# Block-sparse attention with a feed-forward layer on one core: the first eight steps in a new order, weights converted four pieces a step, and the score transposes on TensorE for eight steps and not fourteen

## The chip, the cores and the metric

The kernel runs on one core of one Trainium2 chip. The metric is the device time of one execution in microseconds (us); a kernel's time is the median of its runs. PE is TensorE, DVE is VectorE, ACT is ScalarE, POOL is GpSimd and SP is SyncE, as in the profile.

## The reference

Attention over 4 batches, 8 heads, 768 positions and head size 64, with a mask in blocks of 32, and behind it a layer norm and a two-layer feed-forward with a residual:

```python
scores = (q @ k.T) / sqrt(64)                      # per batch and head, 768 x 768
mask   = |block_i - block_j| <= 1, or block 0 or 23 on either side,
         or one of three sampled blocks of row block i
attn   = softmax(where(mask, scores, -1e9))
x      = (attn @ v), heads side by side            # 4 x 768 x 512, float32
xn     = (x - mean) / sqrt(var + 1e-6) * g_ln
out    = x + relu(xn @ w_ch1) @ w_ch2              # 512 -> 2048 -> 512, weights arrive as float64
```

## The kernel before, in words

**Precision.** Matrix products are made of 16-bit pairs: each operand is split into a rounded high part and the rest as a low part (high by ACT, low by DVE), and three products stand for one: high by high, low by high, high by low.

**Steps.** The attention is cut into 64 steps, 16 for each batch. A sparse step takes one tile of 128 query rows and four heads: scores against 8 key blocks for each row block (`scores`, L324, 96 matmuls). A dense step (16 of the 64) does the row blocks 0 and 23, which see all keys (`dense_scores`, L355, 16 matmuls). Step i then runs: row maximum on DVE (`softmax_max`, L368), exponentials on ACT (`softmax_exp`, L377), a transpose of the 128 x 1024 probabilities, their split in high (ACT, L387) and low (DVE, L394), and the product with V (`attn_v` L431 or `dense_v` L458, called P by V here, 96 or 72 matmuls), whose result DVE divides by the row sums (`finish`, L415 to L418). Steps below `NPE` are early: they are transposed by eight (dense: six) matmuls on PE (`turn`, L382) inside the PSUM tile `ps` that held the scores. Later steps round first (L389, L396) and are transposed by two DMAs on SP's queue (L398), and their P by V is issued `LAG` = 2 steps later. `ps` has two buffers.

**Units.** Twelve units of two query tiles go through `ffn`: 192 matmuls up (L523, 24 for one pair of hidden tiles in PSUM tile `pu`), relu and rounding of a pair on ACT (L531, `hh`) and the rest on DVE (L532, `hl`), then 96 matmuls down (L541, `pd`). `ffn` is a generator: `run(n)` issues its next n pieces, so its matmuls are strewn between the steps' own. Unit 0 holds steps 0 to 3, unit 1 steps 4 to 7, unit 2 steps 8 to 15. A unit is queued behind the one before it.

**Weights.** Both weight matrices come once, in 32 pieces of 512 KB of float64 bits (16 of w1, 16 of w2). `convert_w` makes a piece float32 with three integer operations on DVE (L173, L175, L177, tile `wf`), then rounds it on ACT (`high()`, L187) and forms the low part on DVE (`low()`, L182). Raw pieces wait in three buffers of the pool `raw` or, by the table `HOME`, in eight places inside the final tiles `w2h` and `w2l`, which are filled last. `WPOS` says at which place of which step a piece is converted. `ffn` of unit 0 goes on only with pieces that were written before the step began (`wready`).

**Order.** Nothing is scheduled by a tool: each engine does its instructions in the order in which the code issues them, and an instruction that waits holds all behind it on that engine. The loop at the end writes the order by hand. `hook(i, p)` does what was registered for place p of step i (conversions, gathers) and then lets SP load what is due within ten places. `gather_v` loads the rows of V of a step by DMAs of SP (L290, L294) and up to four indirect ones of POOL (L298); it waits until the buffer `vg` of three steps before has been read by P by V. `gather_k` copies sampled key blocks on ACT (L281). The keys and values of the next batch are converted in steps 7 to 13 (L227, L228, L241, L242).

In an early step the order before is: exponentials of step i, scores of step i+1, feed-forward pieces, `finish` of step i-1, transposes of step i, maximum of step i+1, high and low of step i, P by V of step i. Each early step converts two pieces, or three from step 8 on.

Of the kernel before, what the change touches and what calls it, by code (L numbers as in the profile page):

```python
# [26 lines left out]
def sparse_attention_moe(  # L27
# [28 lines left out]

    ORDER = ((1, 2), (3, 4), (0, 5))
    LAG, FFLAG = 2, 2
    NPE, XPE = 14, 2
    FFU = 192 + 2 * 16 * 6  # L60

    const = ctx.enter_context(tc.tile_pool(name="const", bufs=1))
# [94 lines left out]
    def load_w(i):  # L157
        wraw[i] = stage(i)
        nc.sync.dma_start(wraw[i], weight(i)[0].bitcast(I32))
# [348 lines left out]


    def ffn(u):  # L510
        xT = u.xT
        hh = hp.tile([P, FT, 2 * P], F16, tag="hh", name=f"hh{u.i}")
        hl = hp.tile([P, FT, 2 * P], F16, tag="hl", name=f"hl{u.i}")
        for f in range(0, FT, 2):
            ph = ps_f.tile([P, 512], F32, tag="pf", name=f"pu{u.i}_{f}")
            for j in range(2):
                fs = slice((f + j) * P, (f + j + 1) * P)
                n = 0
                for c in range(CT):
                    for w, k in ((w1h, 0), (w1l, 0), (w1h, 1)):  # L520
                        while u.i == 0 and f // 4 * CT + c not in wready:
                            yield True
                        nc.tensor.matmul(ph[:, j * 2 * P : (j + 1) * 2 * P], w[:, c, fs],  # L523
                                         xT[:, c, k, :], start=n == 0 and j == 0,
                                         stop=n == 3 * CT - 1, skip_group_check=True)
                        n += 1
                        if n < 3 * CT or j == 0:
                            yield
            dh = hh[:, f : f + 2, :].rearrange("p f n -> p (f n)")
            dl = hl[:, f : f + 2, :].rearrange("p f n -> p (f n)")  # L530
            nc.scalar.activation(dh, ph, AF.Relu)  # L531
            nc.vector.scalar_tensor_tensor(out=dl, in0=ph, scalar=0.0, in1=dh,  # L532
                                           op0=ALU.max, op1=ALU.subtract)
            yield

        def down(po, k, f):
            while u.i == 0 and NW1 + f not in wready:
                yield True
            cols = slice(k * P, (k + 1) * P)
            for n, (x, w) in enumerate(((hh, w2h), (hh, w2l), (hl, w2h))):  # L540
                nc.tensor.matmul(po, x[:, f, cols], w[:, f, :], start=f == 0 and n == 0,  # L541
                                 stop=f == FT - 1 and n == 2)

        def store(po, k):
            t = u.ts[k]
            ot = wfp.tile([P, DM], F32, tag="wf", name=f"ot{u.i}_{k}")
            nc.vector.scalar_tensor_tensor(out=ot, in0=po, scalar=1.0 / (SW1 * SW2),
                                           in1=xs[u.b, t], op0=ALU.mult, op1=ALU.add)
            nc.sync.dma_start(out[u.b, t * P : (t + 1) * P, :], ot)

        po = [ps_f.tile([P, DM], F32, tag="pf", name=f"pd{u.i}_{k}") for k in range(2)] if u.i == 0 else []
        if u.i == 0:
            for f in range(FT):
                for k in range(2):
                    yield from down(po[k], k, f)
                    for _ in range(6):
                        yield
            for k in range(2):
                store(po[k], k)
        else:  # L560
            for k in range(2):
                p = ps_f.tile([P, DM], F32, tag="pf", name=f"pd{u.i}_{k}")
                for f in range(FT):
                    yield from down(p, k, f)
                    if f < FT - 1:
                        for _ in range(6):
# [29 lines left out]

    POS = ("pre", "a", "b", "c", "d", "e", "f")
    LEAD = 10

    def place(n):  # L600
        return n + (1 if n < NPE else LAG)

    def matmul_scores(s):
        (dense_scores if s.dense else scores)(s)
# [80 lines left out]
    gather_k(steps[0])  # L685
    for kt in range(3, NT):
        convert_v(0, kt)
    at(0, "a", lambda: convert_k(0, 1, 0))
    at(0, "b", lambda: convert_k(0, 1, 1))
    at(0, "b", lambda: convert_q(0, first[1]))  # L690

    WPOS = [(0, "f")] + [(i, p) for i in range(1, 8) for p in "ab"]
    for i in range(8, 16):
        WPOS += [(i, p) for p in "abf"]
    WPOS = WPOS[:NW]
    assert len(WPOS) == NW
    for i, (n, p) in enumerate(WPOS):
        if i < 3:
            def first_w(i=i):
                convert_w(i)  # L700
                busy["raw"] -= 1
            at(n, p, first_w)
        else:
            item(n, p, HOME.get(i, "raw"), lambda i=i: load_w(i), lambda i=i: convert_w(i))
    for b in range(1, B):
        f = next(s.i for s in steps if s.b == b)
        for kt in range(NT):
# [40 lines left out]
    avail = {}  # L748
    for u in units:
        last = max(s.i for s in steps if s.u is u)  # L750
        avail[u.i] = last + 2 if last < NPE else last + LAG + FFLAG
    need = 0
    i = 0
    tail = None
    while i < NS + LAG + FFLAG + 1 or ffq:
        s = steps[i] if i < NS else None
        for u in units:
# [8 lines left out]
        if i < NPE:  # L766
            if i == 0:
                matmul_scores(s)
                softmax_max(s)
            softmax_exp(s)  # L770
            ahead = 0 < i < NPE - 1
            if ahead:
                matmul_scores(steps[i + 1])
            need -= run(part[0] + part[1])
            hook(i, "a")
            lns = []
            if tail:
                tail()
                lns = norms(steps[i - 1])
            for x in lns:  # L780
                next(x)
            high()
            turn(s)
            if i == 0:
                hook(i, "b")
                keys(1)
            keys(i + 2)
            need -= run(part[2])
            if ahead:
                softmax_max(steps[i + 1])  # L790
            for x in lns:
                next(x)
            hook(i, "b")
            need -= run(part[3])
            split_high(s)
            low()
            for x in lns:
                next(x, 0)
            hook(i, "c")
            split_low(s)  # L800
            high()
            hook(i, "d")
            need -= run(part[4] + part[5])
            tail = matmul_values(s)
            if i == 0:
                matmul_scores(steps[i + 1])
                softmax_max(steps[i + 1])
            hook(i, "e")
            need -= run(part[6])
            low()  # L810
            hook(i, "f")
            high()
            need -= run(part[7])
        else:
            if s:
                matmul_scores(s)
            need -= run(part[0])
            lns = []
            if tail:
                tail()  # L820
                lns = norms(steps[i - 1])
                tail = None
            if s:
                softmax_max(s)
            low()
            hook(i, "a")
            need -= run(part[1])
            if s:
                softmax_exp(s)
            high()  # L830
            need -= run(part[2])
            low()
            hook(i, "b")
            if s:
# [24 lines left out]
            high()  # L859
            need -= run(part[7])  # L860
            low()
# [67 lines left out]
```

## Time and profile before

| | |
|---|---|
| runs | 916.3, 919.24 and 1111.67 us, median 919.24 us |
| profiled execution | 922.66 us, span of its instructions 920.9 us |
| PE busy | 744.5 us (81% of the span) |
| DVE busy | 497.7 us (54%) |
| ACT busy | 468.8 us (51%) |
| DMA moved | 134.08 MB |

The busy shares are means over stages with different limits. The page's second part has the span in 40 slices of 23 us: PE nearly fills its slices from about 253 us on, and does not before. A step is read off the trace by the start of its row maximum (L368 on DVE), the one instruction that each step has once; these starts are the bounds of the windows that the prediction uses.

### The profile page before, as it was taken

What the parts mean: (1) busy time and instruction counts of PE and PEld (TensorE: products, weight loads), DVE (VectorE), ACT (ScalarE), POOL (GpSimd) and SP (SyncE); (2) the same over time, 40 slices, a digit from 0 to 9 for tenths busy, and PEclk for the clock granted to TensorE, in tenths of its full rate; (3) what the DMA queues carried; (4) which work ended last, traced back from release to release, by engine and by line L of the source; (5) the groups of instructions that cost most, each with busy time, mean ns of one, the idle gap of its engine ahead of it and who ended that gap; (6) DMA issues with size and microseconds to landing.
All of it is one profiled execution on the core that took longest, in us unless ns stands there. A gap on an engine that the chain in (4) does not pass through costs nothing.

```text
span 920.9 us, 31832 instructions
## 1 busy us (share of the span) xinstructions
PE 744.5 (81%) x13816; PEld 499.1 (54%) x13816; DVE 497.7 (54%) x900; ACT 468.8 (51%) x1201; POOL 171.8 (19%) x187
## 2 busy tenths in 40 slices
PE   1255584566598899999797899998787999999898
PEld 0133463443366485766554666756544847577483
DVE  4366556889735554554655454546654456435420
ACT  5545434445446565453776565536764664435120
POOL 0522301102001322120222331112122320201000
PEclk9997587787689999999988999999977999999999
DMA  8746632546535887777757887877487785656300
GB/s 286 197 139 186 169 119 90 149 147 206 154 92 106 160 155 168 135 181 176 201 109 163 155 149 174 169 181 195 101 168 165 146 149 138 118 112 123 70 1 23
DMA packets 185419, 134.08 MB, mean 146 GB/s; under 512 B 128960, under 2 KB 164288, under 8 KB 185280
## 3 DMA queue, kind: packets, MB, share of 16 engines
q1 hardware_dynamic: 175872, 108.07, 50.8%
q0 software_dynamic: 8448, 23.44, 10.3%
q8 instruction: 108, 1.77, 0.8%
q10 hardware_dynamic: 960, 0.54, 0.2%
q14 instruction: 31, 0.25, 0.1%
HBM read 89.18 MB, written 12.95 MB: 111 GB/s over the span
## 4 chain that ended last, share of the span: by engine, by line
PE 59%; DVE 13%; issue 8%; ACT 5%; DMA 2%; ACTq 0%; SPq 0%; DVEq 0%
PE pd L541 26%; PE pu L523 21%; PE ps L324 6%; PE pa L431 4%; DVE st L368 2%; DVE hl L532 2%; ACT kg L281 2%; DVE kx L228 1%; DVE wf L175 1%; ACT ps L377 1%; PE pd L458 1%; DVE wf L177 1%; PE ps L355 1%; DVE w2l L182 1%; DMA w2l<-w 1%
## 5 line engine op out<-in xcount | busy, mean ns | idle before, releaser
L298 POOL DMA_INDIRECT vg<-vdr,vidx x176 | 171.2, 973 | 664.7 <-PE pa L431 443.1
L523 PE MATMUL pu<-xT,w1h 128*128 128x256 f16 x1536 | 272.7, 279 | 4.5 <-DVE hl L532 1.8
L523 PE MATMUL pu<-xT,w1l 128*128 128x256 f16 x768 | 214.6, 279 | 0.0
L523 PEld LDWEIGHTS <-w1h 128*128 128x128 f16 x1536 | 153.8, 100 | 30.7 <-issue 4.1
L541 PE MATMUL pd<-w2h,hh 128*128 128x512 f16 x384 | 152.6, 397 | 0.0
L541 PE MATMUL pd<-w2l,hh 128*128 128x512 f16 x384 | 151.5, 394 | 0.0
L541 PE MATMUL pd<-w2h,hl 128*128 128x512 f16 x384 | 150.8, 393 | 0.0
L377 ACT ACTIVATE ps<-ps,st 128x256 f32<-128x256 f32 (+1 forms) x164 | 78.6, 479 | 136.4 <-DVE st L369 132.3
L532 DVE SCALAR_TENSOR_TENSOR hl<-pu,hh 128x512 f16<-128x512 f32 x96 | 65.3, 688 | 111.0 <-ACT hh L531 92.1
L541 PEld LDWEIGHTS <-hh 128*128 128x128 f16 x768 | 73.1, 101 | 88.4 <-issue 13.6
L531 ACT ACTIVATE hh<-pu 128x512 f16<-128x512 f32 x96 | 55.8, 592 | 126.9 <-PE pu L523 107.3
L281 ACT COPY kg<-kx 128x128 f16 x576 | 119.2, 294 | 1.9 <-issue 0.8
L396 DVE TENSOR_TENSOR pw<-ps,pw 128x1024 f16<-128x1024 f32 (+1 forms) x50 | 58.0, 1161 | 106.9 <-ACT pw L389 99.7
L368 DVE TENSOR_REDUCE st<-ps 128x4 f32<-128x1024 f32 (+1 forms) x64 | 73.7, 1151 | 62.9 <-PE ps L324 62.7
L431 PE MATMUL pa<-vg,pt 128*32 128x65 f16 (+1 forms) x4224 | 54.4, 204 | 52.2 <-DVE pt L394 26.4
L431 PEld LDWEIGHTS <-pt 128*32 128x32 f16 x4224 | 45.4, 101 | 71.5 <-DVE pt L394 27.7
L523 PEld LDWEIGHTS <-w1l 128*128 128x128 f16 x768 | 76.9, 100 | 11.7 <-issue 2.0
L324 PEld LDWEIGHTS <-ql 64*32 64x32 f16 x2304 | 34.3, 97 | 71.5 <-issue 47.7
L324 PE MATMUL ps<-kx,ql 64*32 64x96 f16 (+1 forms) x1536 | 44.1, 211 | 35.1 <-DVE ql L265 18.1
L541 PEld LDWEIGHTS <-hl 128*128 128x128 f16 x384 | 38.9, 101 | 49.5 <-issue 7.5
L324 PE MATMUL ps<-kx,qx 128*32 128x96 f16 (+1 forms) x1536 | 45.1, 219 | 10.6 <-issue 10.4
L324 PE MATMUL ps<-kg,ql 64*32 64x96 f16 x768 | 41.4, 216 | 14.5 <-issue 11.3
(80 smaller groups left out, 737.9 us busy)
## 6 DMA issues: line engine op xcount, KB each, us to landing
vg<-vdr SPq DMA_DIRECT2D x32, 390.0 KB
w2l<-w SPq DMA_DIRECT2D x13, 512.0 KB
va<-vdr SPq DMA_DIRECT2D x8, 780.0 KB
w2h<-w SPq DMA_DIRECT2D x12, 512.0 KB
out<-ot SPq DMA_DIRECT2D x24, 256.0 KB
qr<-qs SPq DMA_DIRECT2D x22, 256.0 KB
vdr<-vs SPq DMA_DIRECT2D x36, 130.0 KB
vg<-vdr SPq DMA_DIRECT2D x16, 292.5 KB
```

The lines of the kernel that those rows point to most:

```text
L175: nc.vector.scalar_tensor_tensor(out=wf, in0=raw[:, :, 1], scalar=-0x40000000, in1=wf, op0=ALU.bitwise_and, op1=ALU.bitwise_or)
L281: nc.scalar.copy(kg[:, n], kxs[b, hg][:, :, bass.ds(val, 1)].rearrange("p j o q k -> p j (o q) k"))
L298: nc.gpsimd.indirect_dma_start(vg[:, qb - 4 * s.t, 1, :], None, src[:, :], bass.IndirectOffsetOnAxis(ap=vidx[:, qb : qb + 1], axis=0))
L324: nc.tensor.matmul(dst[:, at : at + n], stat, src[rows], start=first, stop=last, skip_group_check=True)
L368: nc.vector.tensor_reduce(out=s.st[:, 0 : s.m], in_=s.parts, axis=AX.X, op=ALU.max)
L377: nc.scalar.activation(to[:, k], s.parts[:, k], AF.Exp, bias=s.st[:, k : k + 1], scale=0.125)
L396: nc.vector.tensor_sub(s.pw[:, 1, 0 : s.n], s.whole, s.pw[:, 0, 0 : s.n])
L431: nc.tensor.matmul(pa[gr * BLK : (gr + 1) * BLK, hl * 66 : hl * 66 + n], s.pt[:, ch + c, half, gr * BLK : (gr + 1) * BLK], s.vg[:, gr, c, ...
L523: nc.tensor.matmul(ph[:, j * 2 * P : (j + 1) * 2 * P], w[:, c, fs], xT[:, c, k, :], start=n == 0 and j == 0, stop=n == 3 * CT - 1, skip_gr ...
L531: nc.scalar.activation(dh, ph, AF.Relu)
L532: nc.vector.scalar_tensor_tensor(out=dl, in0=ph, scalar=0.0, in1=dh, op0=ALU.max, op1=ALU.subtract)
L541: nc.tensor.matmul(po, x[:, f, cols], w[:, f, :], start=f == 0 and n == 0, stop=f == FT - 1 and n == 2)
```

## The change

`NPE` falls from 14 to 8, so that steps 8 to 13 are transposed by DMA and their P by V comes two steps later. In steps 0 to 7 the order is written anew: P by V of step i-1 stands in step i, behind the transposes of step i, and the scores of step i+1 stand behind that. Pieces 0 to 2 are converted inside step 0, and from step 1 on four pieces a step (places a to d), so that piece 31, the last, stands in step 8 and not in step 13. The feed-forward of unit 0 is queued at step 4, and not 5. In `ffn`, relu and low part of a pair of hidden tiles (`hidden`) are issued when the matmuls of the next pair have been.

```diff
-    NPE, XPE = 14, 2
+    NPE, XPE = 8, 2
...
-            dh = hh[:, f : f + 2, :].rearrange("p f n -> p (f n)")
-            dl = hl[:, f : f + 2, :].rearrange("p f n -> p (f n)")
-            nc.scalar.activation(dh, ph, AF.Relu)
-            nc.vector.scalar_tensor_tensor(out=dl, in0=ph, scalar=0.0, in1=dh,
-                                           op0=ALU.max, op1=ALU.subtract)
+            if late:
+                late.pop()()
+
+            def hidden(f=f, ph=ph):
+                dh = hh[:, f : f + 2, :].rearrange("p f n -> p (f n)")
+                dl = hl[:, f : f + 2, :].rearrange("p f n -> p (f n)")
+                nc.scalar.activation(dh, ph, AF.Relu)
+                nc.vector.scalar_tensor_tensor(out=dl, in0=ph, scalar=0.0, in1=dh,
+                                               op0=ALU.max, op1=ALU.subtract)
+
+            late.append(hidden)
             yield
+        late.pop()()
...
-    WPOS = [(0, "f")] + [(i, p) for i in range(1, 8) for p in "ab"]
-    for i in range(8, 16):
-        WPOS += [(i, p) for p in "abf"]
+    WPOS = [None] * 3 + [(i, p) for i in range(1, 9) for p in PAT.get(i, "abcd")]
...
-        avail[u.i] = last + 2 if last < NPE else last + LAG + FFLAG
+        avail[u.i] = last + 2 - 100 * (u.i == 0) if last < NPE else last + LAG + FFLAG
...
             softmax_exp(s)
-            ahead = 0 < i < NPE - 1
-            if ahead:
-                matmul_scores(steps[i + 1])
-            need -= run(part[0] + part[1])
-            hook(i, "a")
-            lns = []
-            if tail:
+            turn(s)
+            if i == 0:
+                convert_w(0)
+                convert_k(0, 1, 0)
+                split_high(s)
...
+            else:
+                hook(i, "a")
+                high()
+                tail = matmul_values(steps[i - 1])
+                need -= run(part[0] + part[1])
+                hook(i, "b")
+                low()
+                split_high(s)
+                high()
+                split_low(s)
+                if i < NPE - 1:
+                    matmul_scores(steps[i + 1])
                 tail()
                 lns = norms(steps[i - 1])
-            for x in lns:
-                next(x)
-            high()
-            turn(s)
...
+                for x in lns:
+                    next(x)
+                keys(i + 2)
+                need -= run(part[2] + part[3])
+                hook(i, "c")
+                low()
+                high()
+                for x in lns:
+                    next(x)
+                if i < NPE - 1:
+                    softmax_max(steps[i + 1])
+                need -= run(part[4] + part[5])
+                hook(i, "d")
+                low()
...
+                if i == 4:
+                    ffq.append(ffn(units[0]))
+                    need += FFU
+                    need -= run(24)
+                need -= run(part[6] + part[7])
```

Three places show what this does to the order of an engine. First DVE around the low part of step 3 (`pt` is the transposed probability tile, `wf` a weight piece on its way, `w1l` its low part, `st` and `ps` the maximum and scores of a step). Before:

```order
L368 TENSOR_REDUCE st_1365<-ps_1237 128x4
L369 TENSOR_SCALAR st_1365<-st_1365 128x4
L173 TENSOR_SCALAR wf_1368<-w2l 128x512
L175 SCALAR_TENSOR_TENSOR wf_1368<-w2l,wf_1368 128x512
L177 SCALAR_TENSOR_TENSOR wf_1368<-w2l,wf_1368 128x512
L182 SCALAR_TENSOR_TENSOR w1l<-wf_1334,gs,w1h 128x512
L394 TENSOR_TENSOR pt_1372<-ps_935,pt_1372 128x8x128
L182 SCALAR_TENSOR_TENSOR w1l<-wf_1368,gs,w1h 128x512
```

Now:

```order
L173 TENSOR_SCALAR wf_1191<-w2h 128x512
L175 SCALAR_TENSOR_TENSOR wf_1191<-w2h,wf_1191 128x512
L177 SCALAR_TENSOR_TENSOR wf_1191<-w2h,wf_1191 128x512
L173 TENSOR_SCALAR wf_1295<-w2l 128x512
L175 SCALAR_TENSOR_TENSOR wf_1295<-w2l,wf_1295 128x512
L177 SCALAR_TENSOR_TENSOR wf_1295<-w2l,wf_1295 128x512
L182 SCALAR_TENSOR_TENSOR w1l<-wf_1159,gs,w1h 128x512
L182 SCALAR_TENSOR_TENSOR w1l<-wf_1191,gs,w1h 128x512
L394 TENSOR_TENSOR pt_1301<-ps_997,pt_1301 128x8x128
L415 TENSOR_SCALAR rc_2_0_0_1402<-pa_1198 128x4
L416 RECIPROCAL rc_2_0_0_1402<-rc_2_0_0_1402 128x4
L418 TENSOR_TENSOR x_2_1403<-pa_1198,rc_2_0_0_1402 128x256
```

The maximum of step 4 (`st_1365` before) stands ahead of the low part of step 3 (`pt_1372` before, `pt_1301` now) before, and behind these rows now; two pieces' conversions stand directly ahead of the low part.

Second PE where the transposes of step 3 end and P by V begins (`pa` is its result). Before:

```order
L324 LDWEIGHTS qx_3_1036
L324 MATMUL ps_1237<-kg_3_0_1089,qx_3_1036 32x96
L382 MATMUL ps_935<-ident,pw_1232 128x128 x8
L431 LDWEIGHTS pt_1372
L431 MATMUL pa_1384<-vg_823,pt_1372 32x65
```

Now:

```order
L324 MATMUL ps_997<-kg_2_1_825,qx_2_437 32x96
L494 MATMUL px_1_1151<-ident,xn_1_1149 128x128 x4
L382 MATMUL ps_997<-ident,pw_1178 128x128 x8
L431 LDWEIGHTS pt_993
L431 MATMUL pa_1198<-vg_280,pt_993 32x65
```

Before, P by V reads `pt_1372`, the tile that is made from the transposes just ahead of it; now it reads `pt_993`, the tile of step 2. The scores ahead are those of step 4 before, of step 3 itself now.

Third SP from the last gather of an early step on (`va` and `vr` are values, `vdr` their place in memory, `w2l`, `w2h` and `wr` weight pieces on arrival). Before:

```order
L290 DMA vg_1988<-vdr_1_125 96x4x520
L294 DMA vg_1988<-vdr_1_125 32x4x520
L159 DMA w2l<-w 128x1024 x2
L235 DMA vr_0_2317<-v 128x512
L304 DMA va_0_2321<-vdr_0_124 128x6x520
L159 DMA w2l<-w 128x1024
L159 DMA w2h<-w 128x1024 x2
L235 DMA vr_1_2522<-v 128x512
```

Now:

```order
L290 DMA vg_2115<-vdr_1_125 96x4x520
L294 DMA vg_2115<-vdr_1_125 32x4x520
L159 DMA wr_2149<-w 128x1024
L159 DMA w2h<-w 128x1024
L159 DMA wr_2185<-w 128x1024
L159 DMA wr_2187<-w 128x1024
L159 DMA w2l<-w 128x1024
L159 DMA w2h<-w 128x1024
L304 DMA va_0_2504<-vdr_0_124 128x6x520
L235 DMA vr_0_2664<-v 128x512
L159 DMA wr_2693<-w 128x1024
```

From this place on seven weight pieces are still to come now, all shown; before, 19 were, of which five are shown. Each of them waits on SP for the place it is loaded into, and the gathers and value loads stand behind it.

More of the change, by code (lines that the diff above doesn't have):

```diff
@@ L510, in ffn @@
     def ffn(u):
-        xT = u.xT
+        xT, late = u.xT, []
         hh = hp.tile([P, FT, 2 * P], F16, tag="hh", name=f"hh{u.i}")
@@ L598, in sparse_attention_moe @@
     LEAD = 10
+    PAT = {}
     def place(n):
@@ L687, in sparse_attention_moe @@
         convert_v(0, kt)
-    at(0, "a", lambda: convert_k(0, 1, 0))
-    at(0, "b", lambda: convert_k(0, 1, 1))
-    at(0, "b", lambda: convert_q(0, first[1]))
-    WPOS = [(0, "f")] + [(i, p) for i in range(1, 8) for p in "ab"]
-    for i in range(8, 16):
-        WPOS += [(i, p) for p in "abf"]
+    WPOS = [None] * 3 + [(i, p) for i in range(1, 9) for p in PAT.get(i, "abcd")]
     WPOS = WPOS[:NW]
     assert len(WPOS) == NW
[L697 to L704, printed above, removed]
+    for i, at_w in enumerate(WPOS):
+        if at_w:
+            item(*at_w, HOME.get(i, "raw"), lambda i=i: load_w(i), lambda i=i: convert_w(i))
     for b in range(1, B):
@@ L750, in sparse_attention_moe @@
         last = max(s.i for s in steps if s.u is u)
-        avail[u.i] = last + 2 if last < NPE else last + LAG + FFLAG
+        avail[u.i] = last + 2 - 100 * (u.i == 0) if last < NPE else last + LAG + FFLAG
     need = 0
     i = 0
-    tail = None
     while i < NS + LAG + FFLAG + 1 or ffq:
@@ L770, in sparse_attention_moe @@
             softmax_exp(s)
-            ahead = 0 < i < NPE - 1
-            if ahead:
-                matmul_scores(steps[i + 1])
-            need -= run(part[0] + part[1])
-            hook(i, "a")
-            lns = []
-            if tail:
+            turn(s)
[5 more added lines that the diff above has]
+                split_low(s)
+                convert_k(0, 1, 1)
+                keys(1)
+                convert_w(1)
+                convert_q(0, first[1])
+                low()
+                matmul_scores(steps[1])
+                high()
+                convert_w(2)
+                keys(2)
+                softmax_max(steps[1])
+                low()
+                busy["raw"] = 0
+            else:
[6 more added lines that the diff above has]
+                split_high(s)
+                high()
+                split_low(s)
+                if i < NPE - 1:
+                    matmul_scores(steps[i + 1])
@@ L778, in sparse_attention_moe @@
                 tail()
                 lns = norms(steps[i - 1])
-            for x in lns:
-                next(x)
-            high()
-            turn(s)
[L784 to L813, printed above, removed]
+                for x in lns:
+                    next(x)
@@ new lines, in sparse_attention_moe @@
+                keys(i + 2)
+                need -= run(part[2] + part[3])
+                hook(i, "c")
+                low()
+                high()
+                for x in lns:
[4 more added lines that the diff above has]
+                hook(i, "d")
+                low()
+                for x in lns:
+                    next(x, 0)
+                if i == 4:
+                    ffq.append(ffn(units[0]))
+                    need += FFU
+                    need -= run(24)
@@ L814, in sparse_attention_moe @@
+                need -= run(part[6] + part[7])
+                hook(i, "e")
+                hook(i, "f")
         else:
@@ L818, in sparse_attention_moe @@
             lns = []
-            if tail:
-                tail()
+            if i == NPE:
+                matmul_values(steps[i - 1])()
                 lns = norms(steps[i - 1])
-                tail = None
             if s:
```

## The prediction

> **What bounds the kernel now.** I read the page's slices first, then windows cut at the starts of the row maxima, then who waited for whom, then the chain. Columns of a slice row are tenths of 23 us:
>
> ```profile
> PE   1255584566598899999797899998787999999898
> DVE  4366556889735554554655454546654456435420
> PEclk9997587787689999999988999999977999999999
> ```
>
> Two stages are to be seen. From slice 12 (253 us) on PE is at 8 to 9 tenths nearly throughout and DVE at half: there the matmuls set the pace. In the eleven before, PE stands at 1 to 6 tenths but for one 8, its clock from slice 4 on below full, and DVE climbs to 8 and 9 in slices 8 to 10. The early steps and the weights lie in this part, and everything that the change reorders by hand lies ahead of step 19. The issue order behind step 19 is the same in both programs but for the roundings, so the question is when step 19 starts. The markers of steps 2, 9 and 19:
>
> ```profile
> 59.71 1.21 DVE L368 TENSOR_REDUCE st<-ps 128x4 f32<-128x1024 f32 x1
> ...
> 170.83 0.93 DVE L368 TENSOR_REDUCE st<-ps 128x1 f32<-128x768 f32 x1
> ...
> 321.33 1.23 DVE L368 TENSOR_REDUCE st<-ps 128x4 f32<-128x1024 f32 x1 [2.01 <-PE ps L324]
> ```
>
> The windows between markers (columns: bounds, length, busy time of PE, PEld, DVE, ACT, POOL with counts, clock, DMA share, GB/s) are those of steps 3, 5, 10, 11, 12, 13 and 18:
>
> ```profile
> 73.80:88.30 14.50, 8.06 (x205) 5.87 (x206) 9.01 (x17) 7.72 (x25) 3.78 (x4) 0.69 0.54 161
> ...
> 101.70:124.80 23.10, 17.33 (x266) 13.30 (x267) 9.58 (x17) 5.95 (x14) 3.78 (x4) 0.59 0.48 153
> ...
> 186.90:199.10 12.20, 7.21 (x189) 5.49 (x189) 11.78 (x25) 4.65 (x10) 0.00 (x0) 0.86 0.28 70
> 199.10:211.20 12.10, 8.30 (x116) 3.91 (x115) 11.65 (x23) 4.83 (x10) 3.26 (x3) 0.86 0.60 172
> 211.20:224.50 13.30, 8.36 (x112) 4.10 (x111) 11.51 (x23) 4.94 (x12) 2.84 (x3) 0.74 0.73 257
> 224.50:257.70 33.20, 16.74 (x275) 10.08 (x273) 23.47 (x37) 15.64 (x36) 3.98 (x4) 0.68 0.48 145
> ...
> 308.50:321.30 12.80, 11.60 (x235) 6.07 (x234) 3.96 (x7) 7.70 (x21) 3.78 (x4) 1.00 0.86 163
> ```
>
> Step 3 uses neither engine fully: 14.5 us for 9.0 of DVE and 8.1 of PE. Steps 10 to 12, with three pieces a step, are DVE's: 34.9 us busy of 37.6, or 0.93. The waits say why step 3 is loose (first two rows PE's from 0 to 321 us, the others DVE's from 24.3 to 321):
>
> ```profile
> PE pa L431 <- DVE pt L394: 26.4, 9, 4.9
> PE pd L458 <- DVE pt L394: 11.9, 4, 5.0
> ...
> DVE st L368 <- PE ps L324: 32.4, 8, 13.8
> DVE hl L532 <- ACT hh L531: 25.5, 9, 6.0
> DVE hl L532 <- issue: 13.3, 1, 13.3
> ```
>
> P by V waits for the low part of its own step (38 us), the next scores stand behind it on PE, and the maximum on DVE waits for those (32 us): one ring through both engines. The last row is one stall of 13.3 us in step 5, where ACT and DVE stood at a rounding of the feed-forward while PE still ran its pair at half clock.
>
> **The change part by part.** *P by V one step behind.* PE then has the low part ready long before it is asked for, so the two waits of 38 us go. What is late next is DVE, since four pieces a step now stand in its queue. Its prices, from the groups of the first 276 us (after the bar: busy us, mean ns):
>
> ```profile
> L368 DVE TENSOR_REDUCE st<-ps 128x4 f32<-128x1024 f32 (+1 forms) x16 | 18.4, 1149 | 29.5 <-PE ps L324 29.4
> L382 PE MATMUL ps<-ident,pw 128*128 128x128 f32 x104 | 19.0, 341 | 7.7 <-ACT pw L377 7.5
> L394 DVE TENSOR_TENSOR pt<-ps,pt 128x1024 f16<-128x1024 f32 (+1 forms) x14 | 15.9, 1139 | 5.6 <-ACT kg L281 5.6
> L182 DVE SCALAR_TENSOR_TENSOR w1l<-wf,gs,w1h 128x512 f16<-128x512 f32 x16 | 11.8, 743 | 0.0
> L177 DVE SCALAR_TENSOR_TENSOR wf<-w2h,wf 128x512 int32<-128x512 int32 x12 | 8.4, 697 | 0.4
> L532 DVE SCALAR_TENSOR_TENSOR hl<-pu,hh 128x512 f16<-128x512 f32 x10 | 6.9, 688 | 34.2 <-ACT hh L531 20.9 <-issue 13.3
> L173 DVE TENSOR_SCALAR wf<-w2l 128x512 int32<-128x512 int32 x13 | 5.4, 419 | 0.0
> L418 DVE TENSOR_TENSOR x<-pa,rc 128x256 f32<-128x256 f32 (+2 forms) x12 | 5.1, 423 | 0.4
> ```
>
> A piece costs DVE 0.42 + 2 x 0.70 + 0.74 = 2.56 us. *From the maximum of step 2 to that of step 9* the new order has on DVE: 26 triples of integer operations (1.82 each) 47.3 us, 27 low parts 20.1, seven maxima of 1.15 and as many low parts of P of 1.14 16.0, eight `hl` 5.5, and some 54 shorter ones (query parts, `finish`, norms, scalings) at the 0.42 of the last row, 22.7; together about 111 us. At the 0.93 of steps 10 to 12 that is 120 us. Before, the same stretch takes 111 (59.7 to 170.8), with 14 triples in it and not 26: so it becomes longer, not shorter.
>
> *PE in the same stretch.* All of unit 0 moves into it. Prices are read from the chain (start, us, count), at full clock:
>
> ```profile
> 282.61 4.80 PE pu L523 x43
> ...
> 290.86 2.59 PE pd L541 x12
> ```
>
> that is 0.112 us a matmul up and 0.216 down. Between the maxima of steps 6 and 8 the new order has 146 up and 51 down, 27.4 us, and twice a step's own 8.1 us (step 3's row, without feed-forward), 43.6 in all; DVE has 40.5 there, 43.6 at 0.93. The two are even, and two queues that wait for each other now and then lose a little: I add 3 us. The bounds are 0 and, with the clock at half all through, another 27.4.
>
> *Steps 0 and 1.* The scores of step 1 no longer stand behind P by V of step 0, but those of step 2 still stand behind it and the gathers. I leave the maximum of step 2 at 59.7, 8 us either way. The maximum of step 9 then stands at 59.7 + 120 + 3 = 183, against 170.8 before: 12 us are lost here.
>
> *Steps 9 to 18* have no weights any more, and unit 1 alone spread over ten steps: 192 up and 108 down, 45 us, where before units 0 and 1 are crowded into steps 14 to 18. They hold a change of batch, and the profile has two later ones with the same work by the same late code. Steps 28 to 33, then 60 and 61, which carry little feed-forward:
>
> ```profile
> 435.70:449.00 13.30, 11.29 (x237) 8.97 (x236) 9.40 (x18) 8.89 (x21) 4.67 (x5) 1.00 0.83 222
> 449.00:461.40 12.40, 7.82 (x202) 6.31 (x200) 8.56 (x17) 8.37 (x20) 1.64 (x2) 0.88 0.67 170
> 461.40:470.00 8.60, 8.60 (x207) 5.87 (x206) 3.81 (x7) 6.95 (x21) 0.48 (x1) 0.98 0.34 63
> 470.00:477.50 7.50, 5.58 (x108) 3.00 (x107) 5.34 (x13) 6.79 (x20) 3.30 (x4) 0.86 0.50 115
> 477.50:488.60 11.10, 8.35 (x192) 4.37 (x191) 4.80 (x11) 7.59 (x21) 3.78 (x4) 0.94 0.95 191
> 488.60:501.30 12.70, 10.44 (x193) 5.22 (x192) 9.24 (x19) 7.32 (x23) 3.90 (x4) 0.79 0.75 158
> ...
> 823.60:832.40 8.80, 8.80 (x155) 6.84 (x155) 4.81 (x12) 5.14 (x16) 2.84 (x3) 1.00 0.90 192
> 832.40:841.00 8.60, 7.33 (x213) 6.22 (x213) 4.64 (x12) 5.03 (x16) 2.83 (x3) 1.00 0.74 169
> ```
>
> Steps 12 to 17 by the first six: 65.6 us; steps 9, 10, 11 and 18 at 8.7: 34.8; together 100, against 150.5 before (170.8 to 321.3), in which step 13 alone has 33.2: 50 us are won. The bounds are 88 (no step above 8.8) and 128 (each at step 18's 12.8).
>
> *Transposes by DMA in steps 8 to 13.* PE loses 40 matmuls of 19.0 / 104 = 0.18 us, 7 us, on an engine that is not the bound there: no gain. What may come is a wait of P by V for the transfers. Of all late steps one such wait of `pa` is recorded (waits of PE from 321 us on); what SP spends on an issue stands beside it:
>
> ```profile
> PE pa L431 <- DMA pt<-pw: 1.9, 1, 1.9
> L398 SPq DMA_TRANSPOSE pt<-pw x100: 1211/1252/3188, 262.2 to 853.8; - x100
> ```
>
> Bounds 0 and 6 x 1.9 = 11 us; I take 0, since steps 60 and 61 above run at 8.7 us with two such DMAs each.
>
> The Trainium skill speaks against this part: "VectorE: DVE Perf Modes", Rules for kernel authors, advises TensorE for a 128x128 transpose when PSUM will do, and The three transpose paths gives 1309 ns by DMA against 390. By that price the 80 blocks of these steps would take 105 us in a row, where the sum has 52 for steps 9 to 13, and most of what is won would go; this trace, with two such DMAs inside a step of 8.8 us, does not agree.
>
> *Roundings one place later.* The 13.3 us stall goes with step 5's old length, which the sum no longer contains. Behind step 19 PE is the bound and ACT and DVE have room: nothing, 5 us either way.
>
> *Queues behind the moved work.* P by V one step later frees its buffer `vg` one step later; the gather that SP and POOL do into it stands behind that in both queues, and on SP the next weight pieces stand behind the gather. It is read three steps on, as P by V itself moved, so 40 us and more lie between: nothing, and if a gather were missed it would show as a wait of PE (the row of 1.9 us above is the only size that such a wait has there). A rounding that is issued a place later holds its PSUM buffer for one more pair of 24 matmuls, 2.7 us at full clock, while two others of the three are free: nothing.
>
> **The sum.** Step 19 starts at 183 + 100 = 283 instead of 321.3: 38 us less. The profiled execution took 922.66 us, so 884; it was 3.4 above the median of 919.24, so **881** beside that median.
>
> **The rivals.** *The clock stays at half in steps 5 to 8.* For it: 0.59 in step 5 before, though PE was busy 17.3 of 23.1 us. Against it: the clock is 0.98 and 1.00 in the two windows above where PE is busy throughout (steps 30 and 60), and two even engines come near that. Price 27 us: 908. The Trainium skill has the same rule: "TensorE: Matmul & The Clock Gate", Part 1, says that half rate is the default and some 3.4 us of sustained work lift it; by it step 5 starts cold and the later ones do not, which is the 3 us rather than the 27.
>
> *The pieces come too late: slower.* Places of `HOME` are used again half a step after they come free, and SP issues in order, with gathers between. Two pieces were waited for by DVE before (chain, from issue to landing):
>
> ```profile
> 172.97 6.82 DMA w2l<-w
> ...
> 208.50 5.17 DMA w2h<-w
> ```
>
> With half a step of 8 to 10 us ahead of each this stays hidden. If pieces 22 to 31 each held DVE for the 6.82, it would be 68 us on the bounding engine: 881 + 68 = 949, slower. Six such waits (41 us) eat up the gain, and nine (61 us) make it slower by 2%. Against it: four pieces are 2.1 MB, and the window of step 12 moved 257 GB/s at a DMA share of 0.73, which is 8.2 us of a step of 16.
>
> *The light steps are not light.* If something other than the feed-forward keeps each of steps 9 to 18 at 12.8 us, 28 us come back: 909.
>
> *Fuller cover.* DVE without a gap (111) and steps 9 to 18 at 88 give 881 - 9 - 3 - 12 = 857.
>
> **How the numbers follow.** Forecast, 866 to 900: 0.58. Fuller cover: 0.14. Half clock: 0.11. Heavy steps: 0.09. Late pieces: 0.08. The range reaches from fuller cover, less the 8 us of steps 0 and 1, to the half clock: 849 to 909. A measurement tells 2% from no change, which is 901 to 938 here. Half clock and heavy steps come out within it, the late pieces slower, so faster 0.74, within 0.18, slower 0.08.
>
> **What would show it.** Right: no wait of P by V for L394 in steps 1 to 7, DVE over 0.9 busy from 60 us to the maximum of step 9, that maximum near 183, step 19 near 283, and behind it the same 600 us. Wrong: DVE waiting for weight pieces, a clock of 0.6 in steps 5 to 8, or steps 9 to 18 as long as the ones before.

## The result, and the profile after

| | before | after |
|---|---|---|
| median | 919.89 us (4 runs, 916.3 to 1111.67) | 893.36 us (4 runs, 888.18 to 897.74) |
| profiled execution | 922.66 us, span 920.9 us | 896.72 us, span 894.9 us |
| maximum of step 2, 9, 19 | 59.7, 170.8, 321.3 us | 60.5, 182.6, 280.6 us |
| from step 19 to the end | 599.6 us | 614.3 us |

The ratio of after to before is 0.9723, with a 95% interval of 0.9655 to 0.979: faster by 2.8%. One of before's four runs, 1111.67 us, was a slow execution, which the ratio leaves out. The forecast was 881 us, 38 us below before; from 919.24, the median of the other three, to 893.36 it is 25.9 us. In the two profiled executions, too, 26.0 us lie between the spans: 40.7 us were won up to step 19, and 14.7 us lost behind it.

The slices of the page of after, 22.4 us each, which answer to the first rows of the prediction:

```profile
PE   0254486897878999997778999997778999999898
DVE  4679977747654536446553536446463536435420
PEclk9999598998987999998977999998887999999999
```

PE stands at 6 tenths and more from slice 6 on (112 us), where before it did so from slice 12 on; its clock, below 9 tenths in all of slices 4 to 12 before, is so in four of them now (5, 7, 10 and 12). DVE is at 9 in slices 4 and 5, much sooner than before. New are three 7s of PE in a row, twice (slices 19 to 21 and 28 to 30), each with a clock of 7 in or just behind them. The markers of steps 2, 9 and 19:

```profile
60.47 1.22 DVE L368 TENSOR_REDUCE st<-ps 128x4 f32<-128x1024 f32 x1 [2.04 <-PE ps L324]
...
182.61 0.96 DVE L368 TENSOR_REDUCE st<-ps 128x1 f32<-128x768 f32 x1 [0.73 <-PE ps L355]
...
280.64 1.23 DVE L368 TENSOR_REDUCE st<-ps 128x4 f32<-128x1024 f32 x1 [4.34 <-PE ps L324]
```

Windows between steps 2, 9, 19, 32, 48 (columns as in the prediction), first before, then after:

```profile
59.70:170.80 111.10, 66.11 (x1405) 48.90 (x1406) 72.39 (x129) 53.87 (x138) 20.32 (x21) 0.71 0.46 140
170.80:321.30 150.50, 110.58 (x1942) 71.55 (x1941) 100.42 (x177) 81.21 (x211) 22.35 (x23) 0.85 0.58 151
321.30:477.50 156.20, 145.59 (x2827) 101.34 (x2827) 87.01 (x153) 90.23 (x227) 31.12 (x32) 0.98 0.73 161
477.50:670.50 193.00, 174.94 (x3427) 116.38 (x3426) 104.90 (x188) 112.70 (x292) 42.83 (x44) 0.96 0.76 161
```

```profile
60.50:182.60 122.10, 82.27 (x1525) 56.35 (x1526) 103.07 (x181) 63.28 (x156) 21.46 (x22) 0.86 0.53 157
182.60:280.60 98.00, 80.41 (x1773) 51.25 (x1772) 57.92 (x105) 64.89 (x174) 22.67 (x22) 0.88 0.80 175
280.60:441.10 160.50, 147.57 (x2825) 102.12 (x2825) 87.04 (x153) 91.21 (x229) 31.57 (x32) 0.97 0.71 156
441.10:645.00 203.90, 182.90 (x3425) 119.07 (x3424) 105.27 (x189) 112.92 (x292) 42.80 (x44) 0.91 0.75 156
```

The first two rows of each show the gain: 31 us of DVE's work move ahead of step 9, that stretch becomes 11 us longer, and the next one 52.5 us shorter. The last two show the loss, 4.3 and 10.9 us in stretches that issue the same matmuls to within two. In the last row PE is busy 8.0 us longer for them, at a granted clock of 0.91 and not 0.96. PE's waits behind step 19 (us in total, times, longest) name new waits there:

```profile
PE pd L548 <- DVE hl L536: 5.6, 2, 3.0
PE pu L523 <- DVE rc L415: 5.4, 2, 2.8
PE pu L523 <- DVE hl L536: 4.6, 2, 2.3
```

Six waits of 2.3 to 3.0 us, 15.6 in all: three at the change of batch in steps 28 to 32, three in steps 44 to 48. None of the three rows is among the seven longest of before from step 19 on. Before has others at the same places, which after does not have:

```profile
PE pd L458 <- issue: 7.5, 2, 3.9
PE pa L431 <- issue: 1.9, 1, 1.9
PE pa L431 <- DMA pt<-pw: 1.9, 1, 1.9
```

They are waits of P by V. Another view of before, of the transposes by DMA (L398) and of who waited for them, names the two of the first row:

```profile
PE pd L458: 7.5, 2
```

So 15.6 us of waiting took the place of 11.3. With all small gaps PE is idle for 51.1 us behind step 19, where it was 45.9 before (the stretch less PE's busy time): 5.2 of the 14.7 us lost. The other 9.5 are longer busy time, 563.2 us and not 553.7. Of the four waits of before only the two long ones, of 3.6 and 3.9 us, were followed by a clock near half; of the six of after, five were. One of the six in order of time (start, us, engine, line; in brackets the idle time before it and its releaser):

```profile
400.69 2.49 ACT L281 COPY kg<-kx 128x128 f16 x12
...
403.09 0.59 ACT L535 ACTIVATE hh<-pu 128x512 f16<-128x512 f32 x1
...
403.71 0.69 DVE L536 SCALAR_TENSOR_TENSOR hl<-pu,hh 128x512 f16<-128x512 f32 x1 [1.75 <-ACT hh L535]
...
404.45 0.39 PE L523 MATMUL pu<-xT,w1h 128*128 128x256 f16 x1 [2.32 <-DVE hl L536]
```

The relu of a pair, issued one place later, now stands on ACT behind twelve copies of key blocks (for step 30). DVE waits for ACT, and PE, which wants the PSUM buffer, for DVE. The granted clock around this wait (windows; the clock is the third number from the end):

```profile
400.00:402.00 2.00, 2.00 (x28) 1.12 (x25) 1.91 (x2) 1.98 (x8) 1.72 (x1) 1.00 0.74 218
404.40:406.00 1.60, 1.54 (x8) 1.09 (x9) 1.42 (x6) 1.56 (x3) 0.00 (x0) 0.50 1.06 233
406.00:408.00 2.00, 2.00 (x13) 1.49 (x12) 1.94 (x3) 0.39 (x1) 0.00 (x0) 0.62 0.98 232
408.00:410.00 2.00, 2.00 (x84) 1.64 (x83) 1.94 (x4) 0.00 (x0) 0.16 (x1) 1.00 0.45 88
```

PE pays twice: 2.32 us of waiting, and then about 3 us at half clock. The copies alone do not make the wait: twelve of them stand ahead of a relu in other steps too, at 352.93 for one, and no wait of 1.5 us or more follows there. In steps 28 and 29 ACT also converts the next batch's keys (L227, 1.67 us ahead of the copies); in step 30 it does not, and PE waits all the same. What else must come together was not tested.

### The profile page after: what moved, and what is told of

The parts are those of the page before. It is cut to its first block, busy times and chain, and to the rows that moved or that the text cites. A ratio compares the mean times of both kernels' runs of the same rounds, so it can differ in the third digit from the quotient of the medians.

```text
span 894.9 us, 31806 instructions
## 1 busy us (share of the span) xinstructions
PE 742.4 (83%) x13776; PEld 491.1 (55%) x13776; DVE 498.1 (56%) x900; ACT 469.6 (52%) x1201; POOL 173.5 (19%) x187
## 4 chain that ended last, share of the span: by engine, by line
PE 64%; DVE 13%; issue 10%; ACT 8%; DMA 3%; ACTq 1%; SPq 0%; DVEq 0%
PE pd L548 29%; PE pu L523 20%; PE ps L324 8%; PE pa L431 4%; ACT kg L281 3%; DVE st L368 2%; DVE hl L536 1%; ACT ps L377 1%; DVE kx L228 1%; PE pd L458 1%; DVE wf L175 1%; PE ps L382 1%; PE ps L355 1%; DMA w2l<-v 1%; ACT hh L535 1%
## 5 line engine op out<-in xcount | busy, mean ns | idle before, releaser
L523 PE MATMUL pu<-xT,w1h 128*128 128x256 f16 x1536 | 279.9, 284 | 21.6 <-DVE hl L536 10.3
L523 PE MATMUL pu<-xT,w1l 128*128 128x256 f16 x768 | 217.9, 284 | 0.0
L377 ACT ACTIVATE ps<-ps,st 128x256 f32<-128x256 f32 (+1 forms) x176 | 85.7, 487 | 200.5 <-DVE st L369 188.0
L523 PEld LDWEIGHTS <-w1h 128*128 128x128 f16 x1536 | 156.1, 102 | 51.3 <-DVE hl L536 11.9
L396 DVE TENSOR_TENSOR pw<-ps,pw 128x1024 f16<-128x1024 f32 (+1 forms) x56 | 64.3, 1149 | 108.0 <-ACT pw L389 99.7
L324 PE MATMUL ps<-kx,ql 64*32 64x64 f16 (+1 forms) x1536 | 46.3, 205 | 42.5 <-issue 22.6
L324 PE MATMUL ps<-kx,qx 128*32 128x96 f16 (+1 forms) x1536 | 44.4, 220 | 13.8 <-issue 13.8
L324 PEld LDWEIGHTS <-qx 128*32 128x32 f16 x2304 | 36.2, 107 | 32.8 <-issue 29.2
L389 ACT CAST pw<-ps 128x1024 f16<-128x1024 f32 (+1 forms) x56 | 53.3, 951 | 1.6
```

The lines of the kernel that those rows point to most:

```text
L324: nc.tensor.matmul(dst[:, at : at + n], stat, src[rows], start=first, stop=last, skip_group_check=True)
L377: nc.scalar.activation(to[:, k], s.parts[:, k], AF.Exp, bias=s.st[:, k : k + 1], scale=0.125)
L389: nc.scalar.copy(s.pw[:, 0, 0 : s.n], s.whole)
L396: nc.vector.tensor_sub(s.pw[:, 1, 0 : s.n], s.whole, s.pw[:, 0, 0 : s.n])
```

## The experiments

The first theory was that the later rounding alone costs the 10 to 13 us behind step 19; its rival, that this loss is a chance of the clock in one execution. Four versions ran side by side with before, which had a median of 914.14 us there.

**The changed kernel once more** (no edit).

> The changed kernel as it is, timed beside the three that follow, so that they have a partner on the same chip. Both theories: 888 to 898 us, 0.965 to 0.979 of the kernel before.

889.56 us, ratio 0.9727 (0.9698 to 0.9756), span 888.2. Step 19 starts at 280.7, and 607.5 us follow. The loss behind step 19 comes again, though smaller: 7.9 us over before, of which 6.3 are idle time of PE and 1.6 busy time. How much of the clock's share comes thus differs between executions of one kernel.

**The rounding issued at once, in all units.**

```diff
-            late.append(hidden)
+            hidden()
...
-        late.pop()()
```

> The changed kernel with relu and low part of a pair issued at once, as before, for all units. Theory A (the rounding one place later is what lost some 10 us behind step 19: PE waits for a PSUM buffer at the two changes of batch, steps 28 to 32 and 44 to 48): the stretch from step 19 on takes 600 us again and not 614, the PE waits for L536 and L415 there are gone, and the total is 880 to 887, about 10 below the changed kernel; in steps 5 to 8 it may give back up to the 13 us of the old stall, then 885 to 895. Theory B (the 14 us are the clock's chance from run to run): same time as the changed kernel, 890 to 897, within 0.5% of it.

879.22 us, ratio 0.9638 (0.9608 to 0.9669), span 874.5. Step 19 starts at 280.3, and 594.2 us follow. Of PE's waits behind step 19 the longest left are

```profile
PE ps L324 <- issue: 23.7, 41, 1.2
PE pd L458 <- issue: 8.0, 2, 4.0
```

and neither `hl` nor `rc` is among the seven longest. The second row is that of before, come back: part of PE's idle time has moved and not gone. PE is idle for 43.9 us behind step 19 and busy for 550.3, which is 7.2 and 12.9 us less than in after. Without the later rounding step 9 is 6.0 us later (188.6), since some of the old stall at a rounding comes back: step 5 takes 24.7 us (106.0 to 130.7), against 17.5 in after. By step 19 this is made up. In the new order the later rounding thus won nothing that lasts and cost some 10 us.

**The later rounding for unit 0 only.**

```diff
-            late.append(hidden)
+            if u.i == 0:
+                late.append(hidden)
+            else:
+                hidden()
...
-        late.pop()()
+        if late:
+            late.pop()()
```

> The changed kernel with the later rounding kept for unit 0 alone (steps 4 to 9). Theory A: 600 us from step 19 on and step 19 near 281, so 881 to 886. Theory B: as the changed kernel, 890 to 897.

876.3 us, ratio 0.96 (0.9568 to 0.9631), span 879.8: step 19 at 282.9, 596.9 us behind it. It beats both kernels, and lies below the 881 to 886 of the first theory; from the version ahead of it, which is 0.4% slower, it cannot be told. At the same place of the same step, in order of time, ACT and PE (one fence for each engine):

```profile
404.14 2.49 ACT L281 COPY kg<-kx 128x128 f16 x12
406.53 0.59 ACT L535 ACTIVATE hh<-pu 128x512 f16<-128x512 f32 x1
```

```profile
404.33 0.28 PE L523 MATMUL pu<-xT,w1h 128*128 128x256 f16 x1
```

A relu stands behind the twelve copies here too, but it is that of the pair which PE has just ended. The pair ahead of that has been rounded before, so PE starts the next pair at 404.33 without a wait. It does not get through the step without one: P by V behind that pair waits for the transposes by DMA, and the clock falls to half here too (PE in order of time, then a window):

```profile
409.63 1.48 PE L431 MATMUL pa<-vg,pt 128*32 128x65 f16 x72 [2.51 <-DMA pt<-pw]
```

```profile
409.60:412.00 2.40, 2.37 (x77) 2.06 (x78) 2.34 (x3) 0.23 (x1) 0.61 (x1) 0.52 0.48 134
```

The gain shows over the whole of the two changes of batch and not at one wait: steps 28 to 32 and 44 to 48 take 104.5 us together here, and 117.2 in the changed kernel beside it.

**P by V back in its own step** (steps 1 to 7, all else as changed).

```diff
-                tail = matmul_values(steps[i - 1])
...
+                if i == 1:
+                    matmul_values(steps[0])()
+                    norms(steps[0])
+                tail = matmul_values(s)
...
-                lns = norms(steps[i - 1])
+                lns = norms(s)
...
-            if i == NPE:
-                matmul_values(steps[i - 1])()
-                lns = norms(steps[i - 1])
+            if i == NPE and False:
+                pass
```

> The changed kernel with P by V issued in its own step again, right behind the low part and ahead of the next scores, in steps 1 to 7. Theory A (the lag takes a ring off PE and DVE that four pieces a step would not hide): each of seven steps gets longer by the scores that wait for the low part, 1 to 3 us, so step 9 starts at 190 to 203 and the total is 900 to 914. Theory B (DVE is the bound in these steps anyway, the lag is worth nothing): within 3 us of the changed kernel.

907.12 us, ratio 0.9915 (0.9888 to 0.9943), 17.6 us over the changed kernel beside it. Step 2 starts at 66.9 and step 9 at 202.1, 19.2 us later than in the changed kernel. The waits of PE and DVE from 60 to 185 us:

```profile
PE pa L431 <- DVE pt L394: 16.4, 6, 3.7
...
PE pa L431 <- ACT pt L387: 7.9, 3, 2.8
```

```profile
DVE st L368 <- PE ps L324: 12.5, 5, 3.4
DVE rc L415 <- PE pa L431: 12.4, 7, 4.3
```

This is the ring of the prediction, with the rest of the change in place: PE waits for the low and the high part of the same step (16.4 and 7.9 us; after has neither row), and DVE for PE (24.9 us; 6.3 in after).

In the next four, single parts of the change were taken back, or made alone; before had a median of 918.88 us there.

**Weight pieces at the old pace**, two a step and three from step 8 on.

```diff
-[(i, p) for i in range(1, 9) for p in PAT.get(i, "abcd")]
+[(i, p) for i in range(1, 16) for p in PAT.get(i, "ab" if i < 8 else "abf")]
```

> The changed kernel with the weights at the old pace: two pieces a step in steps 1 to 7, three from step 8 on, all converted by step 13. Theory A (the gain comes from the weights' being done by step 8, so that the feed-forward of units 0 and 1 lies in steps 5 to 18 and those steps are light): step 9 starts earlier than 182, at 155 to 170, but steps 9 to 13 are DVE's again at 12 to 13 us and steps 14 to 18 full of feed-forward, so step 19 starts at 300 to 318 and the total is 908 to 926 us against 890 to 897. Theory B (the new order of a step is worth the gain, the pace of the weights little): 885 to 900.

909.56 us, ratio 0.9889 (0.9827 to 0.9952). Step 9 comes sooner (171.3), step 19 later (298.8, against 280.6). So the denser pieces pay: what they cost ahead of step 9 comes back more than twice by step 19.

**Three pieces a step**, so that the last stands in step 10.

```diff
-[(i, p) for i in range(1, 9) for p in PAT.get(i, "abcd")]
+[(i, p) for i in range(1, 12) for p in PAT.get(i, "abc")]
```

> The changed kernel with three pieces a step in steps 1 to 10. Theory A: DVE has 2.5 us less a step up to step 8 and 2.5 more in steps 8 to 10, where it has room; unit 0 ends a step or two later and unit 1 with it: step 9 at 165 to 175, step 19 at 276 to 288, total 885 to 900, close to the changed kernel. Theory B: the same.

898.11 us, ratio 0.9761 (0.9693 to 0.9828): step 9 at 177.8, step 19 at 285.6. The interval covers the changed kernel's 0.9727; between three pieces and four this run doesn't decide.

**`NPE` left at 14**, so that PE transposes steps 8 to 13.

```diff
-    NPE, XPE = 8, 2
+    NPE, XPE = 14, 2
```

> The changed kernel with steps 8 to 13 transposed on PE too (NPE 14). Theory A (PE is not the bound in steps 8 to 13, so 7 us of transposes cost nothing there, and DMA transposes are hidden): step 19 starts within 6 us of 281 and the total is within 1% of the changed kernel. Theory B (the DMA transposes carry part of the gain, as these steps no longer wait on PE for the split): step 14 starts 10 to 25 us later than 229, total 900 to 915.

889.25 us, ratio 0.9679 (0.9611 to 0.9747), against 0.9727 for the changed kernel: step 9 at 175.6, step 19 at 281.4. That step 9 comes 7 us sooner is lost again by step 19, so in the new order the DMA transposes win nothing and cost nothing that these runs can tell.

**Before, with `NPE` at 8 alone.**

```diff
-    NPE, XPE = 14, 2
+    NPE, XPE = 8, 2
```

> The kernel before with NPE 8 alone: old order in steps 0 to 7, old pace of the weights, DMA transposes from step 8 on. Theory A: PE loses 7 us of work where DVE is the bound, and the stall of 33 us at the old change from early to late steps moves or goes: 0.98 to 1.00 of the kernel before. Theory B: 0.955 to 0.975.

908.81 us, ratio 0.9882 (0.9815 to 0.9949). In the old order the same edit is worth 1.2%: step 19 starts at 309.4 and not at 321.3, with 599.7 us behind it. Its worth depends on the other parts, so the parts' gains don't add up.

Four last ones ask whether the later rounding does the same in the old order, and whether anything beats the version that keeps it for unit 0; before had a median of 913.49 us.

**Before, with the later rounding alone.**

```diff
-            nc.scalar.activation(dh, ph, AF.Relu)
...
+            if late:
+                late.pop()()
+
+            def hidden(f=f, ph=ph):
...
+            late.append(hidden)
             yield
+        late.pop()()
```

> The kernel before with one part of the change alone: the roundings (hh on ScalarE, hl on VectorE) issued one place later, in every unit. Theory A (the later rounding takes away the 13 us stall of step 5 and costs 10 to 13 us behind step 19, where two PSUM buffers wait for it at each of the batch changes): the stall in step 5 is gone, PE waits of 2 to 3 us for hl and rc appear behind step 19, and the sum is 0.985 to 1.005 of the time before. Rival (the waits behind step 19 come from the whole new order, not from the rounding): no such waits, only the gain, below 0.985.

912.43 us, ratio 0.9986 (0.9965 to 1.0008): no change. Step 5 takes 13.8 us and not 23.1, so the stall is gone. Step 9 starts at 157.0 and step 19 at 307.2, each 14 us sooner than in the profile of before, and 604.4 us follow, 4.8 more. PE's waits behind 321 us:

```profile
PE pu L523 <- DVE rc L415: 6.6, 2, 4.1
PE pu L523 <- DVE hl L536: 6.1, 3, 2.3
PE pd L548 <- DVE hl L536: 5.5, 2, 2.9
```

These are the same three rows, in the old order: they belong to the rounding and not to the new order. The two spans differ by 9.3 us and the medians by 1.1, because the profiled execution of before was 9.2 us over its median here; how much of the 14 us at the front is real stays open.

**The later rounding for unit 0 only, with `NPE` at 14; with three pieces a step; with unit 0 begun in step 5.** Each takes the version above and one edit more:

```diff
-    NPE, XPE = 8, 2
+    NPE, XPE = 14, 2
```

```diff
-[(i, p) for i in range(1, 9) for p in PAT.get(i, "abcd")]
+[(i, p) for i in range(1, 12) for p in PAT.get(i, "abc")]
```

```diff
-                if i == 4:
+                if i == 5:
```

> The later rounding kept for unit 0 only, and the transposes of P on the DMA queue from step 8 on taken back to TensorE up to step 14. Theory A (the transposes are worth nothing either way, since PE has room in steps 8 to 13): within 5 us of the version with the later rounding for unit 0 only, which ran at 0.960 of the time before: 0.953 to 0.967. Rival (the DMA transposes were worth something that the waits behind step 19 covered): 0.97 or more.

> The later rounding kept for unit 0 only, and three weight pieces a step (through step 11) instead of four (through step 8). Theory A (a piece less a step makes steps 5 to 8 some 5 us shorter and steps 9 to 11 some 10 us longer, whatever the rounding does later): 0.963 to 0.975. Rival (with the rounding mended the pace of the weights no longer decides): 0.955 to 0.962.

> The later rounding kept for unit 0 only, and unit 0's first 24 rows of feed-forward work begun in step 5 instead of step 4. Theory A (in steps 4 to 8 VectorE's queue is nearly full and PE waits for it, so where the 24 rows stand moves work and adds none): 0.953 to 0.967. Rival (the rows fill PE's idle time in step 4, where the granted clock is lowest, and have no such place later): 0.97 or more, with step 19 starting 8 us later or more.

876.12 us (0.9588, 0.9557 to 0.9618), 877.63 us (0.9582, 0.9546 to 0.9619) and 875.52 us (0.9592, 0.9531 to 0.9652). The first and the last came as the first theory had it. With three pieces the rival was right: step 9 comes 5.7 us sooner than with four, and step 19 at 283.0 and 282.9. None of the three can be told from 0.96; with the rounding mended, these runs no longer tell the choices apart.

All profiled executions, by start of step 9, start of step 19, and span less the latter:

| kernel | later rounding | step 9 | step 19 | behind |
|---|---|---|---|---|
| before | no | 170.8 | 321.3 | 599.6 |
| before, `NPE` 8 | no | 182.5 | 309.4 | 599.7 |
| before, later rounding | all units | 157.0 | 307.2 | 604.4 |
| changed | all units | 182.6 | 280.6 | 614.3 |
| changed, again | all units | 182.9 | 280.7 | 607.5 |
| P by V in its own step | all units | 202.1 | 298.9 | 607.4 |
| old pace of pieces | all units | 171.3 | 298.8 | 609.3 |
| three pieces | all units | 177.8 | 285.6 | 609.9 |
| `NPE` 14 | all units | 175.6 | 281.4 | 603.4 |
| rounding at once | no | 188.6 | 280.3 | 594.2 |
| unit 0 only | unit 0 | 185.9 | 282.9 | 596.9 |
| unit 0 only, `NPE` 14 | unit 0 | 175.4 | 278.8 | 592.6 |
| unit 0 only, three pieces | unit 0 | 180.2 | 283.0 | 597.4 |
| unit 0 only, begun in step 5 | unit 0 | 183.4 | 277.8 | 594.6 |

The seven with the later rounding in all units need 603.4 to 614.3 us behind step 19, mean 608.0; the other seven 592.6 to 599.7, mean 596.4. The ranges don't touch, and 11.6 us lie between the means. In the old order alone the two kinds are 4.8 us apart (599.6 and 599.7 against 604.4), in the new order 13.5 (means of 595.1 and 608.6). Two more sums from the same executions say where the 11.6 lie. From the start of step 28 to that of 33 and from 44 to 49, the two changes of batch, the seven with the later rounding need 111.7 to 118.1 us together, mean 115.5, and the others 102.1 to 108.2, mean 104.9: that is 10.6 of the 11.6. And PE is idle behind step 19 for 50.9 to 54.0 us, mean 51.8, against 43.9 to 47.7, mean 45.5: 6.3 of the 11.6, with ranges apart. The other 5.3 are longer busy time of PE, where the ranges overlap (552.5 to 563.2, and 547.9 to 553.7). So the added idle time is shown, and where it lies. That the busy time grows by the half clock behind the waits is read off windows like those above; its size varies from one execution to the next.

## Why the prediction was right, and where it was wrong

*The maximum of step 2* was left at 59.7 and came at 60.5: right.

*From step 2 to step 9*, 123 us were forecast and 122.1 measured, but two errors hide in it. DVE was busy for 103.07 us where the sum had 111. The prices were not at fault: the rows of DVE's groups in this stretch add up to 109.5 us, the 54 shorter ones to 22.8. But an instruction's time in the trace runs a little into the next one's, and the busy time, from which the 0.93 had been taken too, counts such an overlap once. And DVE was busy 0.84 of the stretch and not 0.93. What held PE and DVE there, by PE's and then DVE's waits from 60 to 183 us:

```profile
PE px L494 <- DVE xn L488: 15.5, 4, 7.0
PE ps L382 <- ACT pw L377: 9.6, 4, 3.2
```

```profile
DVE hl L536 <- ACT hh L535: 6.2, 4, 2.0
DVE rc L415 <- PE pa L431: 3.6, 1, 3.6
DVE st L368 <- PE ps L324: 2.7, 3, 2.0
```

P by V no longer waits for L394, as said. In its place PE waits for the layer norm (`xn`), which stands in DVE's full queue, and DVE for the relu on ACT and for PE; its wait ahead of the maximum fell from 32.4 us to 13.0 (from 24 us to step 19). DVE was idle for 19.0 us, where the sum left 12 (9 by the 0.93, and 3 for two queues that wait for each other). That 122.1 lies beside 123 is luck: the two errors, of some 8 and 7 us, cancelled.

*Steps 9 to 18*: 100 forecast, 98.0 measured. The feed-forward spread over ten steps does make them light, and two later batch changes were a good measure of this one. The rival of heavy steps is refuted.

*The clock in steps 5 to 8* did not stay at half. Steps 5 and 8 stand at 0.78 and 0.85; the windows of steps 6 and 7:

```profile
123.60:146.30 22.70, 15.86 (x313) 13.68 (x311) 19.00 (x34) 12.60 (x24) 0.00 (x0) 0.96 0.58 164
146.30:171.10 24.80, 23.77 (x315) 13.68 (x316) 18.66 (x35) 7.20 (x14) 3.72 (x4) 0.89 0.38 124
```

*Late pieces*: among DVE's waits from 60 to 285 us none for a transfer of weights stands in the seven longest rows.

*Transposes by DMA in steps 8 to 13*: taken at 0, and the two pairs with `NPE` at 14 and 8 (0.9679 and 0.9727; 0.9588 and 0.96) differ by less than their intervals. The estimate of 105 us by the price in the Trainium skill, "VectorE: DVE Perf Modes", The three transpose paths, did not appear: steps 9 to 13 took 46.3 us in all (182.6 to 228.9, the start of step 14). No run here times one transfer by itself; what they show is that the transfers lie beside other work. The bound of 11 us was too low, though: the view of L398 from which the prediction has a row lists the two waits of P by V in dense steps as well (7.5 us, above). In after PE waits for none of these transfers.

*Roundings one place later* is **the term that failed**: "nothing, 5 us either way" behind step 19, where 14.7 us were lost in the profile, 7.9 in the second one, and 11.6 between the means of the table. The prediction held that a pair of 24 matmuls, 2.7 us at full clock, would cover the delay, and that ACT and DVE have room. They have on average; at a change of batch ACT's queue had twelve copies in a row (2.49 us), and more ahead of them, before the late relu, and PE waited for that pair's rounding. The prediction looked at the stage's mean load and not at its fullest places. Nor did the sum count the clock: such a wait can be followed by some 3 us at half speed. The window from step 32 to 48 fits this, where PE's own busy time grew by 8.0 us. With 11.6 us on top, the forecast of 881 becomes 892.6, and 893.36 was measured; as the 11.6 were read off afterwards, this says which term was short, and is no test of it. The range held, since it was wide enough for a term that was put at nothing.

*The chances*: by the ones listed for each rival, faster should have stood at 0.72 and within 2% at 0.20, not at 0.74 and 0.18.

## What to carry to other kernels

Giving an engine slack by issuing its consumers later is paid in buffers: before moving an evacuation back, look at the fullest place of the in-order queue that does it, not at that engine's mean load. Apply such a delay only where its stall was seen (here unit 0, and even there these runs cannot tell it from no delay, 0.96 and 0.9638). Price a new wait of TensorE with the half clock that can follow it, and look first whether it takes the place of another wait. Parts of a reordering that each gain in the old order need not add up: those that bring the same step forward can share one gain.

## What the runs showed of the hardware

A wait of 2.32 us was enough to halve the clock for about 3 us (0.50 and 0.62 in the windows above). A longer one, in the same kernel, was not; first PE in order of time, then the window just behind it:

```profile
429.95 0.39 PE L548 MATMUL pd<-w2h,hh 128*128 128x512 f16 x1 [2.60 <-DVE hl L536]
```

```profile
430.00:432.00 2.00, 2.00 (x10) 0.94 (x11) 2.00 (x3) 1.93 (x5) 0.00 (x0) 1.00 0.12 25
```

Over the two changes of batch in all fourteen executions, every wait of PE of 3.4 us and more was followed by a clock near half, and none of 1.5 to 1.95 us was; those of 2.0 to 3.1 us were followed by either.

The Trainium skill, "TensorE: Matmul & The Clock Gate", Part 1, says that the clock falls back after an idle window of some 3.4 us whose start runs free of the program. That the longer wait left the clock at 1.00 and the shorter one halved it agrees with a start that the program does not set; so does the run with three pieces a step, where a wait of 2.31 us at the same place of step 28 left the clock at 1.00. That 2.32 us was enough does not agree with the length given, and here the measurement decides.
